# Gate and up projections as row matmuls with VectorE turns, and fewer, larger weight loads, in a one-token attention + GeGLU layer

## Chip, cores, metric

One core of one Trainium2 chip. The metric is the device time of one execution, in microseconds, median over timed runs. A profiled execution also has a span (first to last instruction), which is 1.75 to 1.97 us shorter than the device time (2.2 to 2.3 us in four of the five runs of e3). Every ratio is of kernels run on the same chip in the same rounds. Where medians of different sets are set side by side (the first result; e1 to e4; e5 to e8; and, on another chip, e9 to e12), the kernel before shows how far the sets agree: 207.70, 207.82, 207.84 and 207.79 us.

## The reference

One token x (640 values) goes through a layer norm, a query projection (640 to 32 heads of 128), attention over a cache of 4,096 keys and values per head, an output projection (4,096 to 640) and a residual. Then a second layer norm and a GeGLU feed-forward of width 1,728:

```python
h  = x + attention(layernorm(x)) @ wo
g  = layernorm(h) @ w_gate            # 640 x 1728
u  = layernorm(h) @ w_up              # 640 x 1728
h2 = h + (gelu(g) * u) @ w_down       # 1728 x 640
```

Everything is bf16. The keys and values are 67 MB of the 84 MB read, so this is in the first place a stream of loads.

## The kernel before

SyncE issues all loads on one queue, in the order wq, x, K and V tiles with w_o pieces between, w_gate, w_up, w_down. TensorE runs a loop of four turns over the heads, then a last stage with the feed-forward. This is the last stage, cut to what matters (DC = 5 row chunks of 128, NFC = 14 column chunks; 1,728 = 13 x 128 + 64):

```python
def up(ps, w, loads):                      # used for gate and for up
    for j in range(DC):
        if j in loads: landed(loads[j])
        for c in range(NFC):               # 70 matmuls: load 128x128 weights, stream ONE column
            PE.matmul(ps[:, c:c+1], lhsT=w[:, j, columns(c)], rhs=hc[:, j:j+1], ...)

for c in range(DC):                        # residual h into y: 20 small fp32 matmuls
    for r in range(YR):
        y_matmul(r, slice(c, YW, DC), hs[:, c:c+1], ident_f[:, 32*r:32*(r+1)], False)
end("g", up(g_ps, wg_sb, {0: "wg0", 3: "wg1"}))
end("u", up(u_ps, wu_sb, {0: "wu0", 3: "wu1", 4: "wu2"}))
PE.wait_ge(S["dve"], D_HID)
# the last 64 rows of w_down lie as half rows on 128 partitions, so hid's last
# 64 values are doubled up by a matmul ("twice") and masked (hid_half)
end("twice", PE.matmul(hid_ps, lhsT=twice[:], rhs=hid[:, FULL:], ...))
# y: 14 chunks x 4 column groups; each waits for its piece of w_down
```

Here hc is h less its mean, as columns, hid is gelu(g) * u, and y is the output row.

The loads of that stage, and of the start:

```python
load("wq0", wq_sb[:, 0:4, :], ...); load("x", ...); load("wq4", wq_sb[:, 4:, :], ...)
...
for i, (a, b) in enumerate(((0, 3), (3, 5))):          load(f"wg{i}", ...)
for i, (a, b) in enumerate(((0, 3), (3, 4), (4, 5))):  load(f"wu{i}", ...)
load("wd0", wd_half, ...)                              # 64 rows as 128 half rows
for i, (a, b) in enumerate(((0, 8), (8, 12), (12, 13))): load(f"wd{i+1}", ...)
```

The softmax here doesn't subtract the row's maximum and nothing guards it: scores larger than these inputs give would overflow.

## Time and profile before

| | before |
|---|---|
| device time, median (12 runs) | 207.70 us (207.51 to 208.00) |
| span of the profiled run | 205.8 us |
| TensorE busy | 76% |
| bytes read | 84.2 MB |
| last piece of w_down landed (first / last of 16 DMA engines) | 199.03 / 202.27 us |

These are lines of the page of the kernel before: span, busy time by engine, then strips of 40 slices (one digit is the busy share of a slice in tenths; PEclk is the granted TensorE clock), then the DMA queues. PE is TensorE's matmuls, PEld its weight loads and PEq its sequencer; DVE is VectorE, ACT ScalarE, POOL GpSimd.

```profile
span 205.8 us, 7931 instructions
...
PE 155.9 (76%) x3713; PEld 150.1 (73%) x3713; DVE 73.9 (36%) x176; ACT 69.9 (34%) x115; POOL 19.6 (10%) x18
...
PE   0015699539974999999999659981999997939673
...
PEclk9999999557975587599589559955595797555555
DMA  5999999999999999999999999999999999999970
...
q8 instruction: 10, 0.16, 0.3%
...
```

The DMA strip is at 9 from the second slice to the one before the last two: the loads never stop, at about 420 GB/s, while TensorE has gaps. So the end of the kernel is the end of the load stream, plus what must follow the last landing. The clock in the last stage is 5 tenths. The queue q8 carries ten instruction packets.

The timeline of the last stage (start, duration, engine, line, operation, out<-in, count, and in brackets the idle time before it and what ended it):

```profile
...
188.84 4.21 PE L434 MATMUL tp<-hc,big 128*128 128x1 bf16 x70
...
193.09 0.23 DVE L649 TENSOR_SCALAR g_sb<-tp,hr 128x14 f32<-128x14 f32 x1 [1.88 <-PE tp L434]
...
195.00 4.20 PE L434 MATMUL tp<-hc,big 128*128 128x1 bf16 x70 [1.95 <-PEq L176]
...
199.24 0.17 DVE L660 TENSOR_TENSOR hid<-g_sb,tp 128x14 bf16<-128x14 f32 x1 [3.87 <-PE tp L434]
...
199.46 0.18 PE L448 MATMUL m<-hid,twice 128*128 128x1 bf16 x1 [0.26 <-DVE hid L660]
...
200.47 1.24 PE L410 MATMUL tp<-big,hid 128*1 128x160 bf16 x32 [0.82 <-PEq L176]
...
201.49 0.35 PE L410 MATMUL tp<-big,hid_half 128*1 128x160 bf16 x4
...
202.00 0.84 PE L410 MATMUL tp<-big,hid 128*1 128x160 bf16 x20 [0.16 <-PEq L176]
202.88 0.32 DVE L666 CAST y_row<-tp 128x160 bf16<-128x160 f32 x1 [2.96 <-PE tp L410]
...
```

The up matmuls take 4.20 us from 195.00; hid is there at 199.4; the detour for the half chunk ends at 199.9; y begins at 200.47 and its last 20 matmuls at 202.00.

The trace also keeps, for each load of weights, keys and values, 16 increments of the load's semaphore with their times; I read them as one for each of the 16 DMA engines and call them landings. TensorE waits for all 16 (`wait_ge(S[name], 16)`). The landings of one load are up to 3.3 us apart (w_up rows 0-2, 191.58 to 194.86). In microseconds:

```
load (before)        first   median  last engine
w_gate rows 3,4      188.48  189.83  190.26
w_up rows 0-2        191.58  192.94  194.86
w_up row 4           193.72  195.07  197.03
w_down rows 0-7      197.03  198.40  200.33
w_down row 12        199.03  200.34  202.27
```

From w_gate to w_up the last engine falls from 0.43 us behind the median to 1.92 us behind, and stays there to the end. Inside that gap, at 192.50, the trace has a 16,384-byte instruction packet that took 1.08 us, and a weight packet of 10,368 bytes that started at 193.57 took 0.85 us where its peers took 0.39. Together they make 1.08 + 0.46 us, which is about the 1.5 us by which the last engine is behind the next; that both were on that engine is inferred, as the trace does not name the engine of a packet.

What these packets are: all ten packets of q8 have 16,384 bytes and took 1.02 to 1.10 us, and the trace ties them to TensorE's program. In the first turn of the loop TensorE stalls as if its next instructions were missing: each stall ends 1.3 to 1.5 us after an instruction packet has ended; these are its TensorE lines around the stalls ("issue" is a wait that the profile cannot name):

```profile
...
32.32 3.32 PE L266 MATMUL s<-q,big 128*128 128x4 bf16 x127
38.13 0.18 PE L266 MATMUL s<-q,big 128*128 128x4 bf16 x1 [2.50 <-issue]
...
45.32 0.21 PE L279 MATMUL o<-ex,big 128*128 128x4 bf16 x2 [3.58 <-issue]
...
59.22 0.28 PE L266 MATMUL s<-q,big 128*128 128x4 bf16 x5 [1.36 <-issue]
...
65.58 0.35 PE L279 MATMUL o<-ex,big 128*128 128x4 bf16 x7 [2.84 <-issue]
...
```

The stalls before 38.13, 45.32, 59.22 and 65.58 lie at instructions 638, 894, 1406 and 1662 of TensorE: multiples of 256 apart. So I read a packet as a block of 256 instructions, and call it a fetch. Seven of the ten packets come by 70.3 us, about the end of the first turn, none in the other three turns, which run the same instructions again, and three in the last stage (185.99, 192.50, 200.10).

### The profile page before, as it was taken

The page shows a single profiled execution, that of the slowest core. Times are in us where ns is not written, and L with a number is a line of the kernel's source. Part 1 is how long each engine was busy: PE and PEld are TensorE (multiplying, and loading weights), DVE is VectorE, ACT ScalarE, POOL GpSimd, SP SyncE. Part 2 cuts the span into 40 slices and gives each one's busy share as a digit, 9 for nine tenths or more (in the row PEclk, how much of TensorE's full clock was granted, in tenths as well). Part 3 has the DMA queues.
Part 4 walks back from the last instruction along what each step waited for, and adds up shares of the span by engine and source line. Part 5 has one row for each costly group of instructions (what it writes and reads, how often), then busy time and mean ns, then how long its engine had stood idle before and what let it go on. Part 6 is the DMA issues. An engine that isn't in the chain of part 4 may idle for free. (4 is left out here: it accounts for less than half of the span.)

```text
span 205.8 us, 7931 instructions
## 1 busy us (share of the span) xinstructions
PE 155.9 (76%) x3713; PEld 150.1 (73%) x3713; DVE 73.9 (36%) x176; ACT 69.9 (34%) x115; POOL 19.6 (10%) x18
## 2 busy tenths in 40 slices
PE   0015699539974999999999659981999997939673
PEld 0011399529974999999999559981999997938672
DVE  7414284006600472382174018400570680114400
ACT  2000173405640274484174416330475565000000
POOL 8300000000000800000350000017000000000000
PEclk9999999557975587599589559955595797555555
DMA  5999999999999999999999999999999999999970
GB/s 197 478 389 433 433 455 449 409 390 470 408 417 468 430 408 414 418 450 439 446 427 420 433 452 412 441 439 414 414 423 427 462 420 414 419 424 421 418 318 5
DMA packets 4918, 84.42 MB, mean 410 GB/s; under 512 B 553, under 2 KB 810, under 8 KB 1322
## 3 DMA queue, kind: packets, MB, share of 16 engines
q1 hardware_dynamic: 4906, 84.23, 96.1%
q8 instruction: 10, 0.16, 0.3%
q14 instruction: 2, 0.02, 0.0%
HBM read 84.23 MB, written 0.00 MB: 409 GB/s over the span
## 5 line engine op out<-in xcount | busy, mean ns | idle before, releaser
L255 PE MATMUL tp<-ident,big 128*128 128x128 bf16 x1024 | 71.2, 242 | 10.5 <-PEq L176 10.5
L255 PEld LDWEIGHTS tp<-ident,big 128*128 128x128 bf16 x1024 | 70.0, 111 | 10.8 <-issue 10.8
L576 DVE COPY big<-tp 128x1024 bf16<-128x1024 bf16 x80 | 53.4, 688 | 48.6 <-PE tp L255 47.6
L551 ACT COPY big<-tp 128x1024 bf16<-128x1024 bf16 x48 | 47.2, 1014 | 56.2 <-PE tp L255 56.2
L279 PE MATMUL o<-ex,big 128*128 128x4 bf16 x1152 | 32.2, 166 | 10.0 <-issue 6.4
L279 PEld LDWEIGHTS o<-ex,big 128*128 128x128 bf16 x1152 | 31.6, 103 | 10.2 <-issue 10.2
L266 PE MATMUL s<-q,big 128*128 128x4 bf16 x1024 | 27.1, 164 | 3.9 <-issue 3.9
L266 PEld LDWEIGHTS s<-q,big 128*128 128x128 bf16 x1024 | 26.9, 96 | 4.0 <-issue 4.0
L485 POOL COPY wo<-wo_in 128x5120 bf16<-128x5120 bf16 x3 | 13.4, 4451 | 122.0 <-PE a L287 122.0
L564 ACT ACTIVATE ex<-s 32x128 bf16<-32x128 f32 x32 | 14.3, 448 | 26.2 <-PE s L266 13.2
L324 PE MATMUL m<-ident,q_row 1*128 1x1 bf16 x5 | 0.3, 172 | 13.4 <-PEq L176 13.4
L324 PEld LDWEIGHTS m<-ident,q_row 1*128 1x128 bf16 x5 | 0.3, 122 | 13.3 <-issue 13.3
L434 PE MATMUL tp<-hc,big 128*128 128x1 bf16 x140 | 8.4, 196 | 1.9 <-PEq L176 1.9
L434 PEld LDWEIGHTS tp<-hc,big 128*128 128x128 bf16 x140 | 8.3, 155 | 2.1 <-issue 2.0
L629 DVE COPY o_raw<-o 128x4 f32<-128x4 f32 x4 | 0.6, 162 | 21.3 <-PE o L279 21.3
L557 ACT CAST q_row<-o 128x512 bf16<-128x512 f32 x1 | 0.6, 586 | 18.9 <-PE o L339 18.9
L569 ACT ACTIVATE e<-t 128x14 f32<-128x14 f32 x1 | 0.2, 214 | 19.9 <-DVE t L652 19.9
L287 PE MATMUL a<-o_row,wo 128*128 128x1 bf16 x160 | 6.9, 178 | 0.0
L614 DVE COPY o_raw<-o 128x4 f32<-128x4 f32 x3 | 0.5, 162 | 17.7 <-PE o L279 17.7
L287 PEld LDWEIGHTS a<-o_row,wo 128*128 128x128 bf16 x160 | 6.7, 131 | 0.0
L564 ACT ACTIVATION_READ_ACCUMULATOR ex<-s 32x1 f32 x32 | 6.5, 202 | 0.4
L198 DVE COPY twice<-ident 128x128 bf16<-128x128 bf16 x1 | 5.0, 5012 | 0.0
(101 smaller groups left out, 60.1 us busy)
## 6 DMA issues: line engine op xcount, KB each, us to landing
big<-in_A_v_cache_dram SPq DMA_DIRECT2D x7, 4096.0 KB, 30.8
big<-in_A_k_cache_dram SPq DMA_DIRECT2D x6, 4096.0 KB, 22.6
big<-in_A_k_cache_dram SPq DMA_DIRECT2D x4, 2048.0 KB, 23.8
wo_in<-in_A_wo_dram SPq DMA_DIRECT2D x4, 1280.0 KB, 26.2
big<-in_A_wq_dram SPq DMA_DIRECT2D x1, 4096.0 KB, 13.0
big<-in_A_v_cache_dram SPq DMA_DIRECT2D x2, 2048.0 KB, 19.8
big<-in_B_w_gate_dram SPq DMA_DIRECT2D x1, 1296.0 KB, 27.3
big<-in_B_w_up_dram SPq DMA_DIRECT2D x1, 1296.0 KB, 33.0
```

Of the source, the lines that this page charges most:

```text
L198: dve(lambda: DVE.tensor_copy(twice[:].rearrange("p (c j) -> p c j", j=2), ident[:, P - LAST :].unsqueeze(2).broadcast_to([P, LAST, 2])), ...
L255: inst = PE.transpose(tp_b[g % NBANK][:, b * DH : (b + 1) * DH], kt[slot][:, g * GRP + b, :], ident[:])
L266: inst = PE.matmul(s_ps[:, j, :], lhsT=kt[slot][:, j, :], rhs=q8[:, slot * QH : (slot + 1) * QH], start=True, stop=True,)
L279: inst = PE.matmul(o_ps, lhsT=vt[slot][:, j, :], rhs=e_t[slot][:, j, :], start=(j == 0), stop=(j == NB - 1))
L287: inst = PE.matmul(attn_ps[:, m : m + 1], lhsT=w[:, j, m::DC], rhs=o_row[:, j : j + 1], start=False, stop=last and j == HG - 1, skip_group ...
L324: inst = PE.matmul(xT[:, c : c + 1], lhsT=x_row[:, c::DC], rhs=ident[0:1, 0:1], start=True, stop=True)
L434: inst = PE.matmul(ps[:, c : c + 1], lhsT=w[:, j, columns(c)], rhs=hc[:, j : j + 1], start=(j == 0 and c == 0), stop=(j == DC - 1), skip_g ...
L485: POOL.tensor_copy(wo_t[:], wo_in[:]).then_inc(S["wo"], 1)
L551: ACT.copy(group(m % SLOTS, g), tp_g[g % NBANK]).then_inc(S["act_pe"], 1)
L557: ACT.copy(q_row[:, 1, :], qr_ps[1][:]).then_inc(S["act"], 1)
L564: inst = ACT.activation(e_t[m % SLOTS][r, :, i], s_ps[r, :, i], AF.Exp, scale=SCALE, accum_out=rs_all[r, h : h + 1])
L576: DVE.tensor_copy(group(m % SLOTS, g), tp_g[g % NBANK]).then_inc(S["dve_pe"], 1)
```

## The change

The intent: make TensorE's part of the last stage short, and give the load queue fewer and wider loads.

- Gate and up: hc (one column) becomes the stationary operand and the weights stream past it, 416 columns in each of four column groups that run side by side; only the last 128 columns keep the old form. 25 matmuls instead of 70. The result lies in rows, so VectorE turns it back into columns with a transpose (this is "the turn" below, not a turn of the loop).
- The last 64 rows of w_down go to partitions 64 to 127 and are used there directly; the half-row detour is gone. The residual is added by VectorE at the end instead of 20 matmuls.
- wq, w_gate and w_up are each one load; w_down is cut 8+3+2 rows instead of 8+4+1.

```diff
-    WD = ((0, 8), (8, 12), (12, 13))
+    WD = ((0, 8), (8, 11), (11, 13))
+    WU = ((0, 5),)
+    RG = FULL * HP                       # 416
...
     def up(ps, w, loads):
-        for j in range(DC):
-            for c in range(NFC):
-                PE.matmul(ps[:, c:c+1], lhsT=w[:, j, columns(c)], rhs=hc[:, j:j+1], ...)
+        for load, a, b in loads:
+            landed(load)
+            for j in range(a, b):
+                for r in range(YR):
+                    PE.matmul(ps[32*r : 32*r+1, 0:RG], lhsT=hc[:, j:j+1],
+                              rhs=w[:, j, r*RG : (r+1)*RG], ..., tile_position=(0, 32*r))
+            for j in range(a, b):
+                PE.matmul(ps[:, RG:RG+1], lhsT=w[:, j, DF-P:], rhs=hc[:, j:j+1], ...)
...
+    def turn_rows(col, ps):
+        rows = ps[:, 0:RG].rearrange("q (p c) -> q c p", c=FULL)
+        dve(lambda: DVE.transpose(col[:, 0:FULL, :], rows), False)
+        dve(lambda: DVE.tensor_copy(col[:, FULL, 0:1], ps[:, RG:RG+1]), False)
...
-    load("wq0", ...); load("x", ...); load("wq4", ...)
+    load("wq", ...); load("x", ...)
...
-    load("wd0", wd_half, B_w_down[FULL*P : DF, :].rearrange("p (a d) -> (p a) d", a=2))
+    load("wd0", wd_last[P-LAST :, :], B_w_down[FULL*P : DF, :])      # 64 rows, partitions 64..127
...
-    for h in "ab": SP.sem_inc(...)       # ahead of the first load on the load queue
+    for h in "ab": ACT.sem_inc(...)
```

More of the change, by code (lines that the diff above doesn't have):

```diff
@@ L55 @@
     LAST = DF - FULL * P
-    WD = ((0, 8), (8, 12), (12, 13))
+    WD = ((0, 8), (8, 11), (11, 13))
+    WU = ((0, 5),)
+    RG = FULL * HP
+    RT = LAST // YR
     EPS = 1e-5
@@ L85 @@
     wd_sb = part(0, FULL * D).rearrange("p (c d) -> p c d", c=FULL)
-    wd_half = part(FULL * D, D // 2)
+    wd_last = part(FULL * D, D)
     ident = sb("ident", [P, P], bf16)
@@ L123 @@
     half_of = sb("half", [P, 2])
-    twice = sb("twice", [P, P], bf16)
+    g_col = sb("g_col", [P, NFC, HP])
+    u_col = sb("u_col", [P, NFC, HP])
+    h_row = sb("h_row", [P, YW])
     hid_half = sb("hid_half", [P, 2], bf16)
@@ L143 @@
     r_ps = m_bank[:, 48 : 48 + HG]
-    hid_ps = m_bank[:, 64:65]
     o_ps = o_bank[:, 0:QH]
-    g_ps, u_ps, y_ps = tp[0][:, 0:NFC], tp[1][:, 0:NFC], tp[2][:, 0:YW]
+    g_ps, u_ps, y_ps = tp[0][:, 0 : RG + 1], tp[1][:, 0 : RG + 1], tp[2][:, 0:YW]
     names = (
         [f"{t}{i}{h}" for t in "kv" for i in range(SLOTS) for h in "ab"]
-        + ["wq0", f"wq{DC - 1}"]
-        + ["x", "wo", "wo_in", "wg0", "wg1", "wu0", "wu1", "wu2", "wd0", "wd1", "wd2", "wd3", "out"]
+        + ["x", "wq", "wo", "wo_in", "wg", "out"] + [f"wu{i}" for i in range(len(WU))] + [f"wd{i}" for i in range(len(WD))]
         + ["pe", "dve", "act", "pool", "q", "dve_pe", "act_pe", "y", "all"]
@@ L171, in wait, with landed @@
             engine.wait_ge(S[which], value)
-    def landed(name):
-        PE.wait_ge(S[name], 16)
-        PE.sem_inc(S[name], -16)
+    def landed(name, n=16):
+        PE.wait_ge(S[name], n)
+        PE.sem_inc(S[name], -n)
     def wait_pe(value):
@@ L197 @@
         dve(lambda: DVE.reduce_sum(col_of[:], by_c.rearrange("p c j -> p j c"), AX.X), False)
-    dve(lambda: DVE.tensor_copy(twice[:].rearrange("p (c j) -> p c j", j=2), ident[:, P - LAST :].unsqueeze(2).broadcast_to([P, LAST, 2])), False)
     dve(lambda: DVE.reduce_sum(half_of[:], ident[:].rearrange("p (c j) -> p j c", j=2), AX.X), False)
@@ L333, in pe_queries @@
         for c in range(DC):
-            if c in (0, DC - 1):
-                landed(f"wq{c}")
+            if c == 0:
+                landed("wq")
             for b in range(2):
@@ L392 @@
     D0 = DVE_Q + 2 * (TURNS - 1)
-    D_SPREAD, D_ROW, D_H, D_HC, D_HID = D0 + 4, D0 + 5, D0 + 7, D0 + 9, D0 + 9 + 14 + 10
+    D_SPREAD, D_ROW, D_H, D_HC, D_HID = D0 + 4, D0 + 5, D0 + 7, D0 + 9, D0 + 9 + 14 + 15
     end = mark_at("end")
@@ L407, with y_matmul @@
     pe_moments(hs, end)
-    def y_matmul(r, at, lhsT, rhs, stop):
+    def y_matmul(r, at, lhsT, rhs, stop, row):
         return PE.matmul(
@@ L416, in y_matmul @@
             skip_group_check=True,
-            tile_position=(0, 32 * r),
+            tile_position=(row, 32 * r),
         )
     PE.matmul(y_ps, lhsT=zero_b[:, 0:P], rhs=zero_b[:, 0:YW], start=True, stop=False, skip_group_check=True)
-    for c in range(DC):
-        for r in range(YR):
-            y_matmul(r, slice(c, YW, DC), hs[:, c : c + 1], ident_f[:, 32 * r : 32 * (r + 1)], False)
-    def columns(c):
-        return slice(c, FULL * P, FULL) if c < FULL else slice(DF - P, DF)
-    def up(ps, w, loads):
-        for j in range(DC):
-            if j in loads:
-                landed(loads[j])
-            for c in range(NFC):
-                inst = PE.matmul(
-                    ps[:, c : c + 1],
-                    lhsT=w[:, j, columns(c)],
-                    rhs=hc[:, j : j + 1],
-                    start=(j == 0 and c == 0),
-                    stop=(j == DC - 1),
-                    skip_group_check=True,
-                )
-        return inst
+    def up(ps, w, loads):
+        for load, a, b in loads:
+            landed(load)
+            for j in range(a, b):
+                for r in range(YR):
+                    PE.matmul(
+                        ps[32 * r : 32 * r + 1, 0:RG],
+                        lhsT=hc[:, j : j + 1],
+                        rhs=w[:, j, r * RG : (r + 1) * RG],
+                        start=False,
+                        stop=(j == DC - 1),
+                        skip_group_check=True,
+                        tile_position=(0, 32 * r),
+                    )
+            for j in range(a, b):
+                inst = PE.matmul(
+                    ps[:, RG : RG + 1], lhsT=w[:, j, DF - P :], rhs=hc[:, j : j + 1], start=False, stop=(j == DC - 1), skip_group_check=True
+                )
+        return inst
@@ L444 @@
+    for ps in (g_ps, u_ps):
+        PE.matmul(ps, lhsT=zero_b[:, 0:P], rhs=zero_b[:, 0 : RG + 1], start=True, stop=False, skip_group_check=True)
     PE.wait_ge(S["dve"], D_HC)
-    end("g", up(g_ps, wg_sb, {0: "wg0", 3: "wg1"}))
-    end("u", up(u_ps, wu_sb, {0: "wu0", 3: "wu1", 4: "wu2"}))
+    end("g", up(g_ps, wg_sb, [("wg", 0, DC)]))
+    end("u", up(u_ps, wu_sb, [(f"wu{i}", a, b) for i, (a, b) in enumerate(WU)]))
     PE.wait_ge(S["dve"], D_HID)
-    end("twice", PE.matmul(hid_ps, lhsT=twice[:], rhs=hid[:, FULL:], start=True, stop=True))
@@ L449 @@
-    down = {FULL: "wd0", 0: "wd1", 8: "wd2", 12: "wd3"}
+    down = {a: f"wd{i}" for i, (a, b) in enumerate(WD)}
     order = list(range(WD[0][1])) + [FULL] + list(range(WD[0][1], FULL))
@@ L452 @@
         if c in down:
-            landed(down[c])
-        if c == FULL:
-            PE.wait_ge(S["dve"], D_HID + 1)
+            landed(down[c], 32 if c == 0 else 16)
         for r in range(YR):
@@ L459 @@
             else:
-                h, w = hid_half[:, r // 2 : r // 2 + 1], wd_half[:, (r % 2) * YW : (r % 2 + 1) * YW]
-            inst = y_matmul(r, slice(0, YW), h, w, i == NFC - 1)
+                h, w = hid[P - LAST :, c : c + 1], wd_last[P - LAST :, r * YW : (r + 1) * YW]
+            inst = y_matmul(r, slice(0, YW), h, w, i == NFC - 1, 0 if c < FULL else P - LAST)
     end("y", inst)
@@ L516, in load_wo @@
         load("wo_in", wo_in[:], src)
-    for h in "ab":
-        SP.sem_inc(S[f"v{SLOTS - 1}{h}"], 16)
-    wq_rows = A_wq.rearrange("(p c) n -> p c n", c=DC)
-    load("wq0", wq_sb[:, 0 : DC - 1, :], wq_rows[:, 0 : DC - 1, :])
+    load("wq", wq_sb, A_wq.rearrange("(p c) n -> p c n", c=DC))
     load("x", x_row, A_x[0])
-    load(f"wq{DC - 1}", wq_sb[:, DC - 1 :, :], wq_rows[:, DC - 1 :, :])
     load_k(0)
@@ L536 @@
     load_wo(TURNS - 1)
-    wg_rows = B_w_gate.rearrange("(p c) f -> p c f", c=DC)
-    for i, (a, b) in enumerate(((0, 3), (3, 5))):
-        load(f"wg{i}", wg_sb[:, a:b, :], wg_rows[:, a:b, :])
+    load("wg", wg_sb, B_w_gate.rearrange("(p c) f -> p c f", c=DC))
     wu_rows = B_w_up.rearrange("(p c) f -> p c f", c=DC)
-    for i, (a, b) in enumerate(((0, 3), (3, 4), (4, 5))):
+    for i, (a, b) in enumerate(WU):
         load(f"wu{i}", wu_sb[:, a:b, :], wu_rows[:, a:b, :])
     SP.wait_ge(S["pe"], pe_at(NQ - SLOTS, "s"))
-    load("wd0", wd_half, B_w_down[FULL * P : DF, :].rearrange("p (a d) -> (p a) d", a=2))
+    load("wd0", wd_last[P - LAST :, :], B_w_down[FULL * P : DF, :])
     wd_rows = B_w_down[0 : FULL * P, :].rearrange("(p c) d -> p c d", c=FULL)
     for i, (a, b) in enumerate(WD):
-        load(f"wd{i + 1}", wd_sb[:, a:b, :], wd_rows[:, a:b, :])
+        load(f"wd{i}", wd_sb[:, a:b, :], wd_rows[:, a:b, :])
     def act_copy(m, g):
@@ L551, in act_copy @@
         ACT.copy(group(m % SLOTS, g), tp_g[g % NBANK]).then_inc(S["act_pe"], 1)
+    for h in "ab":
+        ACT.sem_inc(S[f"v{SLOTS - 1}{h}"], 16)
     ACT.wait_ge(S["pool"], 2 + SLOTS)
@@ L567 @@
         inst.then_inc(S["act_pe"], 1)
-    ACT.wait_ge(S["dve"], D0 + 9 + 14 + 4)
+    ACT.wait_ge(S["dve"], D0 + 9 + 14 + 7)
     ACT.activation(e2[:], t1[:], AF.Exp, scale=TWO_SQRT_2_OVER_PI).then_inc(S["act"], 1)
@@ L629 @@
         event(DVE.tensor_copy(o_raw[:, HG * turn : HG * turn + QH], o_ps))
+    def turn_rows(col, ps):
+        rows = ps[:, 0:RG].rearrange("q (p c) -> q c p", c=FULL)
+        dve(lambda: DVE.transpose(col[:, 0:FULL, :], rows), False)
+        dve(lambda: DVE.tensor_copy(col[:, FULL, 0:1], ps[:, RG : RG + 1]), False)
     assert done["dve"] == D0
@@ L647 @@
     rstd_of(hm, hr)
+    dve(lambda: DVE.transpose(h_row[:].rearrange("q (p c) -> q c p", c=DC), hs[:, 0:DC].unsqueeze(2).broadcast_to([P, DC, HP])), False)
     wait_pe(T["end", "g"])
-    dve(lambda: DVE.tensor_scalar(g_sb[:], g_ps, hr[:], None, op0=ALU.mult))
+    turn_rows(g_col, g_ps)
+    dve(lambda: DVE.tensor_scalar(g_sb[:], g_col[:, :, 0], hr[:], None, op0=ALU.mult))
     dve(lambda: DVE.tensor_tensor(t1[:], g_sb[:], g_sb[:], op=ALU.mult))
     dve(lambda: DVE.tensor_scalar(t1[:], t1[:], GELU_C, 1.0, op0=ALU.mult, op1=ALU.add))
-    assert dve(lambda: DVE.tensor_tensor(t1[:], t1[:], g_sb[:], op=ALU.mult)) == D0 + 9 + 14 + 4
+    assert dve(lambda: DVE.tensor_tensor(t1[:], t1[:], g_sb[:], op=ALU.mult)) == D0 + 9 + 14 + 7
     DVE.wait_ge(S["act"], ACT_ALL)
@@ L659 @@
     wait_pe(T["end", "u"])
-    assert dve(lambda: DVE.tensor_tensor(hid[:], g_sb[:], u_ps, op=ALU.mult)) == D_HID
-    wait_pe(T["end", "twice"])
-    assert dve(
-        lambda: DVE.tensor_scalar(hid_half[:], half_of[:], hid_ps, None, op0=ALU.mult), False
-    ) == D_HID + 1
+    turn_rows(u_col, u_ps)
+    assert dve(lambda: DVE.tensor_tensor(hid[:], g_sb[:], u_col[:, :, 0], op=ALU.mult)) == D_HID
     wait_pe(T["end", "y"])
-    DVE.tensor_copy(y_row[:], y_ps).then_inc(S["y"], 1)
+    DVE.tensor_tensor(y_row[:], y_ps, h_row[:], op=ALU.add).then_inc(S["y"], 1)
     SP.wait_ge(S["y"], 1)
```

## The prediction

> **What bounds it now.** The load stream. The page's DMA strip is 9 tenths in slices 2 to 38, at about 420 GB/s (84.2 MB); TensorE is busy 76% and waits for data. The last stage, from the timeline and the landing times in the trace:
>
> - w_gate landed at 190.26 us (last of 16 engines), w_up at 194.86, 195.97 and 197.03, w_down at 197.22, 200.33, 201.86 and 202.27. The median engine landed the last piece at 200.34: one engine is about 1.5 us behind the next (200.78).
> - That engine fell behind between 190.3 and 194.9. In that gap the trace has a 16 KB instruction packet (192.50 us, 1.08 us long), and a weight packet beside it took 0.85 instead of 0.39. [...] TensorE stalls in the first turn of the loop lie exact multiples of 256 instructions apart, and 10 such packets are in the instruction queue.
> - w_up's 70 matmuls ran 195.00 to 199.20, hid at 199.24, the half-chunk detour to 199.92, y 200.47 to 202.84 with its last 20 matmuls after 202.00, the copy of y 0.32, the output DMA, end at 205.8.
>
> So the critical end is: last landing, 0.6 us of matmuls, 0.32 us copy, output. TensorE's gate and up work (4.2 us each) is mostly hidden behind loads.
>
> **What the change does.**
> - gate and up: 70 weight loads of 128x128 with one moving column each become 20 row matmuls of 416 columns (four column groups) and 5 full ones. The query projection, same form, took 0.425 us for four 512-wide ones at half clock, so 5 x 0.35 + 0.4 = about 2.2 us instead of 4.2 (estimate; granted clock is 0.50 there).
> - Added on VectorE, twice: a 128x416 fp32 turn and a copy, 0.75 us (estimate from the 0.69 us copy of 128x512 fp32 from PSUM). Removed: the half-chunk detour (0.7 us), 40 small residual matmuls (0.8 us, hidden), and a 5 us setup copy (hidden).
> - hid then at about 199.0, a little sooner than now; y can start as w_down lands.
> - [...] Two semaphore instructions leave the head of the load queue: 0.1 us.
> - x now lands behind all of wq: the first turn starts about 3 us later (x landed 13.27, wq 16.61). Hidden: the loads queued by 5 us last until 47.6 to 49.4, and the next is issued at 38.4, so 41.6 still keeps the queue fed.
> - About 220 fewer TensorE instructions after the loop. Counting 256-blocks, the fetch now at 192.5 is asked for when the up matmuls begin (about 195.6) and runs at 198 to 200. If it falls on an engine still loading w_down, the last landing stays near 202.0; if not, it is near 200.7.
>
> **Time.** With the delayed engine, TensorE ends near 202.4 instead of 202.84: 207.15 us. Without, near 201.3: 206.1 us. I put 60% on the first: 206.7 us, 80% range 205.9 to 207.4. Faster by over 2%: 0.02; within 2%: 0.97; slower: 0.01.
>
> **What would show it.** DMA share still 9 tenths to slice 38; gate and up about 2.2 us each; hid near 199; y's last matmuls right after the last landing; no tail fetch at 192 to 193; the first transposes near 28 us without a gap in DMA near 48.
>
> **What would make it wrong.** A gap in the load stream from the later start; a slow turn (strided fp32 in PSUM); another instruction fetch on a late engine; row matmuls that don't overlap, making up cost over 4 us.

Two passages are cut: a statement on how instructions are fetched that did not come from the runs, and the term for fewer and wider loads, for which no measurement was named. With that term in it the sum came to 207.15 us with the delayed engine and 206.1 us without, and 0.6 and 0.4 of them make 206.7. The term for the queue head can be read in the trace of the kernel before: there the two semaphore instructions start at 0.95 and 1.03 us and the first load at 1.11, 0.16 us after the first of them. The time of the next fetch was my estimate, counted in blocks of 256 from the stalls above.

## The result

| | before | changed |
|---|---|---|
| device time, median | 207.70 us (12 runs, 207.51 to 208.00) | 206.63 us (8 runs, 206.45 to 206.68) |
| span of the profiled run | 205.8 us | 205.4 us (second profile: 204.7) |

The ratio is 0.9947, with a 95% interval of 0.9937 to 0.9957. (A ratio is the mean time of one kernel's fast runs over that of the other's of the same rounds, so it is not quite the ratio of the medians above.) The change gains 1.1 us, half a per cent. Two more runs of the changed kernel, 207.31 (profiled) and 206.99 us, are not among the eight. By the spans the gain is 1.3 us (206.0, the median of the kernel before in the rounds of e1, to 204.7).

The page of the changed kernel, first profile:

```profile
span 205.4 us, 7665 instructions
...
PE 153.4 (75%) x3584; PEld 144.3 (70%) x3584; DVE 75.4 (37%) x179; ACT 70.1 (34%) x115; POOL 19.6 (10%) x18
...
DMA  7999999999999999999999999999999999999980
...
q8 instruction: 9, 0.15, 0.3%
...
```

The DMA strip is full as before, and the later arrival of x (landed at 15.6 us instead of 13.3) opened no gap in it. The instruction queue has nine packets, one fewer. The last stage:

```profile
...
190.75 1.90 PE L429 MATMUL tp<-big,hc 128*1 128x416 bf16 x20 [1.95 <-DVE rs_w L220]
...
192.58 0.29 PE L439 MATMUL tp<-hc,big 128*128 128x1 bf16 x5
...
196.65 2.19 PE L429 MATMUL tp<-big,hc 128*1 128x416 bf16 x20 [3.77 <-PEq L179]
...
198.76 0.29 PE L439 MATMUL tp<-hc,big 128*128 128x1 bf16 x5
199.09 0.62 DVE L629 STREAM_TRANSPOSE u_col<-tp 128x416 f32<-128x416 f32 x1 [3.21 <-PE tp L439]
199.63 0.12 DVE L630 COPY u_col<-tp 128x1 f32<-128x1 f32 x1
199.79 0.18 DVE L664 TENSOR_TENSOR hid<-g_sb,u_col 128x14 bf16<-128x14 f32 x1
...
200.11 2.23 PE L412 MATMUL tp<-big,hid 128*1 128x160 bf16 x56 [1.06 <-PEq L179]
...
202.40 0.33 DVE L666 TENSOR_TENSOR y_row<-tp,h_row 128x160 bf16<-128x160 f32 x1 [2.43 <-PE tp L412]
...
```

Gate takes 2.1 us instead of 4.2 (190.75 to 192.87), up 2.4 us (196.65 to 199.05), the turn and its copy take 0.7 us, and y's 56 matmuls run from hid to the end without a gap.

This first profile is of an execution that took 207.31 us, above all timed runs. In it w_gate's last engine landed at 190.66, 1.1 us behind the median, where all later profiles with w_gate in one load have 0.3 to 0.8; the instruction packet of 186 us probably fell on the engine that was last already, though the trace does not name the engine. I ran the same kernel again (e1) and read the changed kernel from that profile.

### The profile page after: what moved, and what is told of

It reads as the page before. It is cut to its first block, busy times and chain, and to the rows that moved or that the text cites. A ratio compares the mean times of both kernels' runs of the same rounds, so it can differ in the third digit from the quotient of the medians.

```text
span 205.4 us, 7665 instructions
## 1 busy us (share of the span) xinstructions
PE 153.4 (75%) x3584; PEld 144.3 (70%) x3584; DVE 75.4 (37%) x179; ACT 70.1 (34%) x115; POOL 19.6 (10%) x18
## 5 line engine op out<-in xcount | busy, mean ns | idle before, releaser
L257 PE MATMUL tp<-ident,big 128*128 128x128 bf16 x1024 | 72.6, 245 | 7.7 <-PEq L179 7.7
L257 PEld LDWEIGHTS tp<-ident,big 128*128 128x128 bf16 x1024 | 71.4, 112 | 7.9 <-issue 7.9
L326 PEld LDWEIGHTS m<-ident,q_row 1*128 1x128 bf16 x5 | 0.3, 122 | 15.6 <-issue 15.6
L429 PE MATMUL tp<-big,hc 128*1 128x416 bf16 x40 | 4.1, 543 | 5.7 <-PEq L179 3.8
L429 PEld LDWEIGHTS tp<-big,hc 128*1 128x1 bf16 x40 | 1.3, 108 | 7.8 <-issue 7.8
L202 DVE CAST ident_f<-ident 128x128 f32<-128x128 bf16 x1 | 4.8, 4822 | 0.0
```

The costliest lines, as they stand in the source:

```text
L202: dve(lambda: DVE.tensor_copy(ident_f[:], ident[:]), False)
L257: inst = PE.transpose(tp_b[g % NBANK][:, b * DH : (b + 1) * DH], kt[slot][:, g * GRP + b, :], ident[:])
L326: inst = PE.matmul(xT[:, c : c + 1], lhsT=x_row[:, c::DC], rhs=ident[0:1, 0:1], start=True, stop=True)
L429: PE.matmul(ps[32 * r : 32 * r + 1, 0:RG], lhsT=hc[:, j : j + 1], rhs=w[:, j, r * RG : (r + 1) * RG], start=False, stop=(j == DC - 1), ski ...
```

## The experiments

My theory: the gain comes from the load stream. The fetch that held back one engine by about 1.5 us left the last loads, because TensorE's program got shorter; and the end follows the last landing. Rival A: the shorter work of TensorE is the gain. Rival B: the new grouping of the loads is the gain.

Landings in all profiles, in us, with the time of the ninth instruction fetch. The device time is the median of the timed runs, while the landings are of the one run profiled, which in e3 was the slowest of its five (208.51):

```
                          w_up complete    last w_down      9th fetch   device us
                          median  last     median  last
before                    195.07  197.03   200.34  202.27   192.50      207.70
after, first profile      195.02  196.51   200.52  201.68   201.97      207.31 (this run)
e1_again (changed)        195.09  195.82   200.57  200.96   201.27      206.6 (206.63)
e9_again_timed (changed)  195.04  195.92   200.44  201.08   201.38      206.68
e2_loads_only             194.68  196.82   199.96  202.04   194.14      208.47
e3_fetch_back             195.00  197.53   200.47  202.68   192.40      208.04
e4_wu_split               195.15  196.12   200.54  201.28   205.46      206.86
e5_rows_only              195.45  196.01   200.79  201.21   201.94      206.96
e6_wd128                  194.88  195.21   200.34  200.68   201.76      206.25
e7_early                  195.41  195.94   200.45  200.99   201.29      206.90
e8_wd128_wu_split         194.78  195.54   200.27  201.01   203.77      206.56
e10_wd128_again           194.83  195.44   200.30  200.91   201.48      206.43
e11_wd128_one_row         194.71  195.19   200.19  200.66   201.89      206.45
e12_slow_hid              195.17  196.05   200.69  201.24   205.96      206.88
```

### e1_again: the changed kernel, a second profile

No edit that changes the program.

> The changed kernel once more, unchanged in what it does, for a second profile. In its first profile (a run of 207.31 us, where the timed runs gave 206.6) every load packet between 192.9 and 196.2 us took 20 to 25% longer than elsewhere. If that slow stretch belongs to the kernel, it comes back and the span is 205.4 us with the last landing at 201.7. If it was a disturbance of that one run, no packet is slow, the last landing is near 201.0 and the span near 204.7.

Measured: 206.6 us, span 204.7, last landing 200.96. TensorE in the last stage:

```profile
...
190.20 1.90 PE L429 MATMUL tp<-big,hc 128*1 128x416 bf16 x20 [1.45 <-PEq L179]
192.03 0.29 PE L439 MATMUL tp<-hc,big 128*128 128x1 bf16 x5
195.96 2.17 PE L429 MATMUL tp<-big,hc 128*1 128x416 bf16 x20 [3.64 <-PEq L179]
198.06 0.29 PE L439 MATMUL tp<-hc,big 128*128 128x1 bf16 x5
199.42 2.23 PE L412 MATMUL tp<-big,hid 128*1 128x160 bf16 x56 [1.06 <-PEq L179]
```

But the slow stretch was there again. So of the two alternatives written down neither held as a whole: the stretch belongs to the kernel, and the 0.7 us of the first profile came from an engine that was late, not from the stretch. How slow the packets are, mean of the packets of 10,240 bytes that started between 193 and 196 us:

```
before 385 ns    changed, first profile 489    e1_again 481    e2_loads_only 387    e6_wd128 393    e7_early 387
```

### e2_loads_only: the grouping of the loads alone

```diff
 # on the kernel before
+ wq, w_gate, w_up in one load each; WD = ((0, 8), (8, 11), (11, 13)); sem_inc moved to ACT
```

> The kernel before with the new grouping of its loads alone (wq, w_gate and w_up each in one load, w_down in 8+3+2 rows, two semaphore instructions off the load queue), gate and up still 70 matmuls each. My theory (the delayed engine sets the end[...]): the instruction fetch still runs near 192.5 and still delays one engine, 207.4 us or slower, as gate and up now wait for a whole matrix before they start 4.2 us of work. Rival (the grouping of the loads is what gave 1 us): 206.7 us.

Measured: 208.47 us, ratio 1.0022 (1.0008 to 1.0037), slower than before. The fetch ran at 194.14, and the last landing was 202.04. The loads themselves did become quicker: the median engine ended at 199.96 instead of 200.34. But the old up work now waits for the whole of w_up and starts at 196.95, ends at 201.2, and y follows it without a gap:

```profile
...
190.25 4.20 PE L434 MATMUL tp<-hc,big 128*128 128x1 bf16 x70 [1.50 <-issue]
196.95 4.21 PE L434 MATMUL tp<-hc,big 128*128 128x1 bf16 x70 [2.50 <-PEq L176]
...
201.55 1.24 PE L410 MATMUL tp<-big,hid 128*1 128x160 bf16 x32
...
```

Rival B falls: the grouping alone loses. There the end is no longer the last landing but TensorE's chain, which a one-piece load makes longer. That chain began late because of the delayed engine as well: w_up was complete at 196.82, on the next engine at 195.35. So e2 shows the grouping together with the fetch, not the grouping by itself.

### e3_fetch_back: the fetch put back among the last loads

```diff
 # on the changed kernel, before the gate matmuls, into a free PSUM bank
+    for _ in range(50):
+        PE.matmul(tp[3][:, 0:1], lhsT=zero_b[:, 0:P], rhs=zero_b[:, 0:1], start=True, stop=True, ...)
```

> The changed kernel with 50 dummy matmuls of one column put in front of the gate matmuls, where TensorE waits for w_gate anyway (about 3 us of work that ends about when w_gate lands). They move the place where TensorE's program enters its next 256-instruction block back to about 188.5 us, so the instruction fetch that ran at 202 in the changed kernel runs again at 191 to 193, amid the last loads. My theory: one engine is delayed by up to 1.5 us, last landing up to 202, time 207.2 to 207.7 us if the engine is a late one, little change if it is an early one. Rival (TensorE's shorter work in the last stage is what gave 1 us): at most 0.3 us slower than the changed kernel, 206.6 to 206.9.

(The place of the next block and the time of the fetch are my estimates, counted in blocks of 256 as in the prediction.)

Measured: 208.04 us, 1.4 us slower than the changed kernel (206.63), a little slower than before (1.0007, 0.9992 to 1.0021, so no clear difference). The dummies took 1.52 us, not 3, and cost no time themselves: the gate matmuls start at 190.35, and in e1 at 190.20, with w_gate landing 0.16 us later.

```profile
...
188.69 1.52 PE L447 MATMUL tp<-zero_b 128*128 128x1 bf16 x50
190.35 1.90 PE L429 MATMUL tp<-big,hc 128*1 128x416 bf16 x20
...
197.66 1.90 PE L429 MATMUL tp<-big,hc 128*1 128x416 bf16 x20 [5.18 <-PEq L179]
199.50 0.29 PE L439 MATMUL tp<-hc,big 128*128 128x1 bf16 x5
200.85 2.40 PE L412 MATMUL tp<-big,hid 128*1 128x160 bf16 x56 [1.06 <-PEq L179]
```

The fetch ran at 192.40 and took 1.10 us; a 17,280-byte weight packet at 193.48 took 1.21 us, where others took 0.64, or up to 0.77 at that time. First and median landings are those of e1 (w_up median 195.00 against 195.09), and only the last engine is 1.7 us later (197.53 against 195.82). All of the 1.7 us passes to the last landing (202.68 against 200.96). These are of the slowest run of e3; the median span is 205.8 us (205.7 to 206.3), 1.1 us above the changed kernel's 204.7. The other 0.3 us of the 1.4 lies outside the span, where e3 spends 2.2 us and the changed kernel 1.9, for a cause that was not looked for. In device time the effect was larger than I had written down. In this form w_up comes in one piece, so the late engine holds up the up matmuls, the turn and y, one after the other.

Since TensorE's useful work is that of the changed kernel, with no time added, rival A cannot explain 208.04 us. The fetch is shown to be worth about 1.1 us of span here (1.4 us of device time), enough for most of the gain of 1.3 us of span. That e3 is level with the kernel before, though, hides a balance: e3 has the new slow stretch of loads and the new TensorE form, which before has not.

### e4_wu_split and e12_slow_hid: does the time from w_up to hid matter?

```diff
 # e4, on the changed kernel
-    WU = ((0, 5),)
+    WU = ((0, 3), (3, 5))
 # e12, on e4: the turn done twice
     turn_rows(u_col, u_ps)
+    wait(DVE, "dve", done["dve"]); turn_rows(u_col, u_ps)
```

> The changed kernel with w_up in two loads again (rows 0 to 2, rows 3 and 4). Three of the five groups of row matmuls can run before the rest lands, so hid is ready about 0.8 us sooner[...]. If the end waits for the last landing (my theory) the time stays within 0.2 us of 206.6. If TensorE's and VectorE's work after w_up sets it (rival; in the first profile the 56 last matmuls ran without a gap from hid on), it falls by 0.5 us or more, to 206.1 or below.

> The changed kernel with w_up in two loads, with the turn of the up rows on VectorE done twice (0.75 us more between the up matmuls and hid, no TensorE instruction added). In the run without it, hid stood ready at 198.2 us and y waited for w_down until 199.4. My theory (the last landings set the end): unchanged, 206.6 to 206.9 us. Rival (the time from w_up to hid is what the change gained): 0.75 us slower, 207.4 us or more.

Measured: e4 206.86 us (ratio 0.9946), e12 206.88 us (0.9957, intervals 0.9932 to 0.9960 and 0.9943 to 0.9971). The median of e4 is 0.26 us above 206.6, just outside the 0.2 that I had written down; its ratio is that of the changed kernel. VectorE in e4, then in e12 (the first lines end with hid, the last is the add of the residual to y):

```profile
...
197.99 0.18 DVE L664 TENSOR_TENSOR hid<-g_sb,u_col 128x14 bf16<-128x14 f32 x1
201.91 0.32 DVE L666 TENSOR_TENSOR y_row<-tp,h_row 128x160 bf16<-128x160 f32 x1 [3.73 <-PE tp L412]
...
```

```profile
...
198.46 0.12 DVE L630 COPY u_col<-tp 128x1 f32<-128x1 f32 x1
198.62 0.18 DVE L666 TENSOR_TENSOR hid<-g_sb,u_col 128x14 bf16<-128x14 f32 x1
201.86 0.32 DVE L668 TENSOR_TENSOR y_row<-tp,h_row 128x160 bf16<-128x160 f32 x1 [3.06 <-PE tp L412]
...
```

hid ends at 198.17 in e4 and at 198.80 in e12, and y's add comes at 201.91 and 201.86. Having hid 1.1 us sooner than e1 (199.27) won nothing, and taking 0.63 us of that back cost nothing: with w_up in two loads the end waits for w_down, whose first eight rows landed at 199.34 and 199.30 and whose last at 201.28 and 201.24. In the form as changed the two limits are close: y ran from 199.42 to 201.65 without a gap and ended 0.69 us after the last landing at 200.96. In e4, where the last eight matmuls (0.46 us) do wait for the landing, y ended 0.57 us after it (201.85 against 201.28). So the two limits are about 0.1 us apart.

### e5_rows_only: the new compute with the old loads

```diff
 # on the changed kernel
+ wq 4+1 with x between, w_gate 3+2, w_up 3+1+1, w_down 8+4+1; sem_inc back on SP
```

> The changed kernel's compute with the old grouping of the loads (wq in 4+1 rows with x between, w_gate 3+2, w_up 3+1+1, w_down 8+4+1, the two semaphore instructions back at the head of the load queue). If the new compute form, with its 220 fewer TensorE instructions, is what gains (my theory), the time is 206.6 to 206.9 us and no instruction fetch runs between 190 and 196. If the grouping were needed for the gain, 207.2 us or more. The slow stretch of load packets near 193 to 196, which all profiles of the changed form show and those with the old compute do not, should be there, since the last 64 rows of w_down are still loaded to 64 partitions.

Measured: 206.96 us, ratio 0.9962 (0.9950 to 0.9975). The fetch ran at 201.94, after the last landing (201.21), and the slow stretch was there as expected (453 ns, measured as under e1). The time is just above the 206.6 to 206.9 that I expected. So the compute form with its shorter program brings about 0.8 of the 1.1 us (0.38% of 207.8); the new grouping, which loses alone, seems to add about 0.3 us once the up work is short enough to follow a one-piece load. The intervals of e5 and of the changed kernel (0.9937 to 0.9957) overlap, so this 0.3 us is not clear of noise.

### e6_wd128, e7_early, e10_wd128_again: the slow stretch

```diff
 # e6 and e10, on the changed kernel
-    load("wd0", wd_last[P-LAST :, :], B_w_down[FULL*P : DF, :])    # 64 rows on 64 partitions
+    load("wd0", wd_last[:], B_w_down[DF-P : DF, :])                # 128 rows on 128 partitions
 # e7, on the changed kernel: own buffer, the 64-partition load ahead of w_gate
```

> The changed kernel with the last piece of w_down loaded as its last 128 rows to all 128 partitions instead of its last 64 rows to partitions 64 to 127 (80 KB more, of which the upper half is not used). If the 64-partition load makes the slow stretch of 193 to 196 us (each engine lost about 0.5 us in it), the stretch is gone and the last landing is 0.3 us earlier in spite of 80 KB more (0.2 us): 206.3 us or a little over, as y's matmuls then set the end. If the stretch comes from something else, it stays and the last landing is 0.2 us later: 206.8 us.

> The changed kernel with the 64-row piece of w_down in a buffer of its own and loaded just ahead of w_gate instead of between w_up and w_down. If that load causes the slow stretch, the stretch moves to where that load is processed, near 182 to 186 us, and the last landing is as before: 206.6 us. If the slow stretch belongs to the time or to what the engines compute then, it stays at 193 to 196.

> The last 128 rows of w_down on 128 partitions, a second time: 206.25 us as in its first runs, 0.3 to 0.4 us below the changed kernel in the same rounds, no slow stretch near 193 to 196. If its first result was chance, 206.6 us.

Measured: e6 206.25 us (ratio 0.9933), e10 206.43 us (0.9937), e7 206.90 us (0.9958; 0.3 us above what I expected, with a last landing of 200.99 as in e1). e10 is 0.25 us below e9 of the same rounds, where I expected 0.3 to 0.4. The windows of e1, e6 and e7 (stretch and its length in us; busy time and count of PE, PEld, DVE, ACT and POOL; granted clock, DMA share, GB/s):

```profile
...
182.00:186.00 4.00, 2.91 (x88) 2.80 (x89) 0.62 (x3) 0.00 (x0) 0.00 (x0) 0.50 1.05 444
188.00:192.00 4.00, 2.55 (x23) 0.55 (x20) 2.92 (x17) 0.00 (x0) 0.00 (x0) 0.50 1.00 428
192.00:196.00 4.00, 0.36 (x11) 0.28 (x8) 2.42 (x11) 0.22 (x1) 0.00 (x0) 0.50 0.98 359
...
```

```profile
...
182.00:186.00 4.00, 2.96 (x89) 2.82 (x90) 0.62 (x3) 0.00 (x0) 0.00 (x0) 0.50 1.02 435
...
192.00:196.00 4.00, 0.92 (x19) 0.46 (x19) 2.42 (x11) 0.22 (x1) 0.00 (x0) 0.50 0.98 405
...
```

```profile
...
182.00:186.00 4.00, 2.35 (x74) 2.24 (x74) 0.62 (x3) 0.00 (x0) 0.00 (x0) 0.50 1.03 388
...
192.00:196.00 4.00, 1.01 (x17) 0.22 (x9) 2.39 (x11) 0.22 (x1) 0.00 (x0) 0.50 0.97 414
...
```

The DMA share stays at 0.97 to 1.05 throughout, so the engines are hardly ever idle; only the GB/s shows the loss. In e1 192 to 196 moved 359 GB/s; with the last rows on 128 partitions it moved 405; with the 64-partition load put ahead of w_gate it moved 414, and the dip went to 182 to 186 (388, where e1 has 444). The dip follows that load, so that load makes it. It is 80 KB, but packets of other loads are slow too: in e1 its own packets ran from 192.96 to 195.29 us, and the slow packets lie between 193.3 and 196.0. The load packets between 193 and 196 us lost about 8 us of engine time against their usual durations, 0.5 us for each engine; in e6 and e10 they lost 0.4 us in all.

Why that load costs time, whether by the number of its partitions or by which they are, and how the loss spreads to packets of other loads, is not shown. (The 0.2 us for 80 KB more in the text of e6 is an estimate, 80 KB at the measured 420 GB/s.)

### e8_wd128_wu_split and e11_wd128_one_row: further steps

```diff
 # e8, on e6:  WU = ((0, 3), (3, 5))
 # e11, on e6: WD = ((0, 8), (8, 12), (12, 13))
```

> The last piece of w_down on 128 partitions and w_up in two loads, together. With the slow stretch gone the loads end about 0.3 us sooner and hid is ready before w_down lands, so both limits of the end move: 206.2 us. If the slow stretch stays, 206.8 us.

> The same with w_down cut 8+4+1 as in the kernel before, instead of 8+3+2: four matmuls instead of eight follow the last landing, about 0.2 us less (8 took 0.47 us at half clock)[...]. If the last landing sets the end, 206.1 us; if y's matmuls run without a gap from hid on, no change.

> The changed kernel once more, timed in the same rounds as the variants of this call, so that they can be compared with it on one chip: 206.6 us, 0.5% below the kernel before.

Measured: e8 206.56 us (0.9942), e11 206.45 us (0.9937), e9 206.68 us (0.9946). Neither e8 nor e11 brought what I had expected. In e8 hid was early and the stretch was gone, but the last engine landed at 201.01, 0.33 us later than in e6. It was already 0.24 us later when the last V piece landed (182.09 against 181.85), before any part of the change. e11's last landing was 200.66, as in e6. The spread of the 16 engines at the start of the last stage thus differs between profiles by about 0.3 us, for a cause that I did not find, and it is as large as what these steps could win.

The best version is the changed kernel with the last 128 rows of w_down on all partitions: 206.25 and 206.43 us in two sets of five runs, against 206.63 and 206.68 for the changed kernel. The intervals of the ratios overlap (0.9923 to 0.9950 and 0.9932 to 0.9959, both in the rounds of e9), so its 0.2 to 0.4 us is small and not clear of noise by the time alone; what supports it is that the rate in the stretch recovered in every profile with it (401 to 415 GB/s from 192 to 196 us in e6, e8, e10 and e11, against 359 and 360 in e1 and e9).

## Why the prediction was right or wrong

The time was right: 206.63 us against 206.7, inside 205.9 to 207.4, and within 2% as given. Point by point:

- **The bound.** Right. The DMA strip stayed full, and e4 and e12 show that the end follows the landings when w_up comes in two loads. In the form as changed, TensorE's chain from w_up ends about 0.1 us later than that.
- **The delayed engine.** Right by the landings: with the fetch at 192.5 one engine was 1.93 us behind the median at the end, without it 0.39 (e1), and putting a fetch back at 192.4 cost 1.4 us, 1.1 of it within the span (e3).
- **When the fetch would run.** Wrong, and this is the step that failed: "asked for when the up matmuls begin (about 195.6) and runs at 198 to 200". In all profiles with the new compute and no dummies it ran between 201.3 and 206.0, after the last landing or after y. I gave 60% to the branch in which it delays an engine; the other came. Counting blocks of 256 says which fetch disappears from the busy part, not when the next one runs: in e4, e8 and e12 it ran at 203.8 to 206.0, in the others at 201.3 to 202.0, and I do not know what triggers it. The traces do show a count: TensorE had executed 7,227 instructions (weight loads, matmuls and the sequencer's own, all turns) when the ninth fetch began in the kernel before, 7,233 in e2, and 7,234 to 7,244 in all profiles with the new compute and no dummies, whose whole programs have 7,243 to 7,247. So the fetch came at about the old count, and the shorter program reaches that count only at its end. That this is the trigger is not shown: e3 (7,172) and the tenth fetches (158 and 105 instructions after the ninth in the kernel before and in e2, not 256) do not fit.
- **The landing without the delay.** Predicted 200.7, measured 200.96 and 201.08 (e1, e9; 201.68 in the first profile). The time for that branch was put at 206.1 and came out 206.6. One missing term probably explains most of it: the slow stretch that the 64-partition load causes, 0.5 us per engine. Without it e6 and e10 landed at 200.68 and 200.91 and took 206.25 and 206.43 us. I named other risks and not this one. So the central figure was near the result because two misses, the late fetch (gain) and the slow stretch (loss), partly cancelled.
- **Loads.** The sum had too little for them: with the loads alone the median engine ended 0.38 us sooner (e2). The first load was issued at 0.96 instead of 1.11 us, as predicted to 0.05.
- **Gate and up.** About 2.2 us each predicted, 2.1 and 2.4 measured. (The "half clock" of the query projection is inferred from its own groups, which started 0.43 us apart and from 22.2 us on 0.22; the trace's record of the granted clock begins at 22.08 us only, so it does not show that clock.) The turn and copy: 0.75 predicted, 0.7 measured. hid near 199.0: 199.27.
- **x later.** Predicted 3 us without effect. It was 2.3 us (15.6 against 13.3), first transposes of the loop at 28.0 us in e1 against 25.2, no gap in the load stream.
- **y right after the last landing.** Only nearly: y ran without a gap from hid, and ended 0.69 us after the last landing, where e4, which waits for that landing, took 0.57.

A balance for the last landing, 202.27 to 200.96 (-1.31 us): the fetch out of the way about -1.5 (the last engine's lag behind the median was 1.93 us before and is 0.39 in e1), the loads -0.4 (median, e2), the slow stretch +0.6 (median, e1 against e2). The sum is -1.3, as it must be, since the three are taken from the same landings; it is no test of the parts. Against e6, which loads 80 KB more (0.2 us, an estimate from the measured 420 GB/s), e1 is only 0.23 us later in the median, so of the +0.6 about 0.4 belongs to the slow stretch and the rest is not explained. What the old compute form would cost without the fetch was not tried. Dummies in the kernel before, as in e3, might have moved its fetch, and would have tested rival A from the other side.

## What to carry to other kernels

Where a kernel ends with its load stream, look at the landings of the single DMA engines, not at the mean DMA share: from first to last landing of the last load it was 3.2 us in the kernel before, with the fetch, and 1.75 us in e1. Here one engine that was late after an instruction fetch of 16 KB delayed the whole kernel by about 1.1 us of span (e3), so fewer instructions in the last stage can be worth more than the engine time that they take. Try merging loads where the work behind the merged load is short: here the same grouping lost 0.5 us with 4.2 us of up work behind it (and a delayed engine before it), and seemed to gain 0.3 us with 2.4 us. In a busy stream look at small loads that do not fill the 128 partitions: reading a few rows twice here kept the rate up where a 64-partition load did not (405 GB/s in e6 against 359 in e1, from 192 to 196 us), for 0.2 to 0.4 us that is not clear of noise by the time alone.
